# Ten extra products on squared tokens, a higher recording rate for attention pieces, and the second pair's row factors computed apart

## The chip, the cores and the metric

The kernel runs on one core of a Trainium2 chip. Its time is the device time of one execution in microseconds (us); the figure used is the median of several executions. The engines are PE (matmul), DVE (vector), ACT (activation), POOL (GpSimd) and SP, which here only issues DMAs.

## The reference

Attention with normed q and k, then two expert layers, all in fp32:

```
q_n = q / sqrt(mean(q*q) + 1e-6) * g_q          # 4 batches, 12 heads, 448 tokens, 64 wide
k_n = k / sqrt(mean(k*k) + 1e-6) * g_k
a   = softmax(q_n @ k_n.T / 8) @ v              # heads joined: x is 1792 x 768
h   = x @ w_in;  x2 = where(h > 0, h, exp(min(h, 0)) - 1) @ w_out            # 768 -> 2048 -> 768
xn  = x2 / sqrt(mean(x2*x2) + 1e-6) * rms_g
out = (silu(xn @ w_gate) * (xn @ w_val)) @ w_out2                            # 768 -> 1536 -> 768
```

## The kernel before

**Tiles.** Heads are taken two at a time: a pair i (0 to 23) belongs to batch i // 6. A weight or an activation is held as a rounded high part and a low remainder, and a product of two such values is three matmuls of 448 columns (`mm3`). Weights come packed in 8 bytes a value and are unpacked by ACT or POOL and DVE (`w_convert`), kept in DRAM, and split by ACT or POOL and POOL or DVE (`w_split`).

**Stages.** First the lead-in: attention of pairs 0 to 5 alone. Then five stages of expert work: stage 0 is the first experts of batch 0, stage 1 the first experts of batch 1, stage 2 the second experts of both, stages 3 and 4 the same for batches 2 and 3. Attention of later pairs is recorded between the expert units, in pieces. A pair has 15 pieces: four score groups (`s_group`, 0 to 3), eight transposes (`t_bank`) and three parts of the product with v (`pv`). `GOALS` says how many pairs' pieces have been recorded at the end of each stage, and a stage's rate is the pieces still wanted divided by its units (40 in stages 0 and 1). With 12 the rate of stage 0 is (180 - 90) / 40 = 2.25 pieces a unit, and batch 1's last pair, pair 11, is recorded with stage 0's last unit. Stage 1 needs the result of pairs 6 to 11 (`split_x` makes the tiles `xs` from it).

**What a pair does.** `load_tk` brings its q and k rows (`tk`, 480 KB), ACT squares them (`squares`), DVE sums them into `ss`, and `factors` turns sums into the row factors `rr` by some twelve small DVE instructions. `load_rw` brings q and k transposed (`rw`); `prep_q` and `prep_k` split them into high and low parts, after k has been multiplied by its factors spread over the partitions (`rb`). `spread` makes `rb`: for pairs below `FIRST` by eight small matmuls into a PSUM bank, for the others by a DMA to DRAM (`scr`) and two back. Then come scores into a bank, a row maximum on DVE (`nm`), an exponential on ACT with its row sum, transposes through PE, copies, products with v, and a last multiplication by the reciprocal sums, which also travel through DRAM (`rsum`, `rsb`). In the lead-in pairs 1, 3 and 5 put their tiles into storage that is idle then, so the same thing is called `wr` or `gbig` (raw q, k and their parts), `tbig` (p), `ybig` (transposed p, and the tokens of pairs 2 and 3). The tokens of pair 1 and 5 lie in `wr`; those of pairs 0, 4, 6 and all later ones share one tile `tk`, so a load waits until the pair before has been read.

**What sets the order.** Every operation is recorded in a list (`Plan.add`) with a price and the engines that may do it. `Plan.schedule` then plays the list through with these prices, ready operations that were recorded first going first, and gives each engine a fixed order. On the chip each engine works through its own order, and the DMA queue of SP through its own.

**PSUM.** In the lead-in banks 0 to 3 take scores (`r_s`), 4 to 6 transposes (`r_t`), and bank 7 alone takes the spread factors and the output of `pv`. In the order below bank_129 is bank 0 and bank_136 is bank 7.

Of the kernel before, what the change touches and what calls it, by code (L numbers as in the profile page):

```python
# [20 lines left out]
CW = 6  # L21
NF1 = 4
NF2 = 4
FIRST = 1

# [193 lines left out]
def kernel(ctx: ExitStack, tc: tile.TileContext, dims, tok, qk, vr, gq, gk, wst, rmsg, ident_in, out):  # L221
    nc = tc.nc
    B, H, S, D, CF1, CF2 = dims
    NPB = H // 2
# [40 lines left out]
    def size(ap):  # L265
        n = 1
        for s in ap.shape[1:]:
            n *= s
        return n
# [4 lines left out]
    def c_v1(n):  # L274
        return 0.15 + 0.00104 * n
# [7 lines left out]
    def mm(o, l, r, start, stop, price=None):  # L283
        n = size(r)
        plan.add(
            {"pe": (price or max(0.108, n / 2400.0 + 0.017), lambda: T.matmul(o, l, r, start=start, stop=stop))},
            [o], [l, r] + ([] if start else [o]), lag=0.17,
        )
# [70 lines left out]
    def act(dst, src, func, extra=0.0, accum=None, after=None, **kw):  # L359
        if accum is not None:  # L360
            kw["accum_out"] = accum
        plan.add(
            {"a": (c_a(size(src)) + extra, lambda: A.activation(out=dst, in_=src, func=func, **kw))},  # L363
            [dst, accum], [src] + [x for x in kw.values() if hasattr(x, "tensor") and x is not accum], after=after,
        )

    def vop(price, fn, outs, ins, after=None):
        plan.add({"v": (price, fn)}, outs, ins, after=after)
# [4 lines left out]
    def dma(dst, src, nbytes, after=None, soon=False, by="sp"):  # L373
        q, cost = (SP, 0.4) if by == "sp" else (A, 0.2)
        plan.add(
            {by: (cost, lambda: q.dma_start(out=dst, in_=src))},  # L376
            [dst] if dst.name != out.name else [], [src], lag=nbytes / Plan.DMA_RATE, after=after, soon=soon, dma=True,
        )


    ident = sb.tile([P, P], F32, name="ident")
# [52 lines left out]
    r_s, r_t, r_o, r_m = Ring(), Ring(), Ring(), Ring()  # L434
# [93 lines left out]
    def rsqrt(y, x, t, scale, eps):  # L528

        ts(x, x, scale, eps, ALU.mult, ALU.add)  # L530
        yi = y.bitcast(I32)
        ts(yi, x.bitcast(I32), 1, None, ALU.logical_shift_right)
        ts(yi, yi, -1.0, float(0x5F3759DF), ALU.mult, ALU.add)
        ts(x, x, -0.5, None, ALU.mult)
        for _ in range(3):
            tt(t, y, y, ALU.mult, "v")
            tt(t, t, x, ALU.mult, "v")
            stt(y, t, 1.5, y, ALU.add, ALU.mult)

    def tk_of(i):  # L540
        return tks[i % 4 if i < NPB else 0]

    def load_tk(i):
        b, k = divmod(i, NPB)
        if k == 0:
            norms[b] = (r_ss.next(), r_rr.next())
        dma(tk_of(i), tok[i], P * 15 * D * 4)

    def squares(i):

        b, k = divmod(i, NPB)
        tk, ss = tk_of(i), norms[b][0][:, 15 * k:15 * k + 15]
        act(tk, tk, AF.Square)
        tk3 = tk.rearrange("p (t d) -> p t d", d=D)
        vop(c_v1(15 * D), lambda: V.reduce_sum(out=ss, in_=tk3, axis=AX.X), [ss], [tk])

    def factors(b, k0, k1):

        c = slice(15 * k0, 15 * k1)
        ss, rr = norms[b]  # L560
        rsqrt(rr[:, c], ss[:, c], r_sn.next()[:, c], 1.0 / D, 1e-6)

    def spread(i):
# [3 lines left out]
        rr = d["rr"] = norms[b][1][:, 15 * k:15 * k + 15]  # L567
        if i < FIRST:
            rb = d["rb"] = r_o.next()
# [15 lines left out]
    def load_rw(i):  # L585
        dma(l_rw.of(i), qk[i], P * 1024 * 4)

    def load_v(i):
        d = AT.setdefault(i, {})
        t = r_rv.t[i % 2]  # L590
        dma(t, vr[i], P * 512 * 4)
        d["v"] = t.rearrange("p (t d) -> p t d", d=D)

    def prep_q(i):
        d = AT.setdefault(i, {})
        rw, qh, ql = (l.of(i)[:, 0:512] for l in (l_rw, l_qh, l_ql))
        copy(qh, rw)
        tt(ql, rw, qh, ALU.subtract)
        d["q"] = (qh, ql)

    def prep_k(i):
        d = AT[i]
        rw, kh, kl = (l.of(i)[:, 512:1024] for l in (l_rw, l_qh, l_ql))
        stt(rw, rw, gsc[:, 0:1], d["rb"], ALU.mult, ALU.mult)
        copy(kh, rw)
        tt(kl, rw, kh, ALU.subtract)
        d["k"] = (kh, kl)
# [125 lines left out]
    PIECES = 15  # L733

    def tail(i, u):
        t_bank(i, u)
        yield
        if u in (3, 5, 7):
            pv(i, (2, 3) if u == 7 else ((u - 3) // 2,))
            yield  # L740

    def attention():
        load_tk(0)
        load_rw(0)
        load_consts()
        for i in range(1, 4):
            load_tk(i)
        squares(0)
        factors(0, 0, 1)
        spread(0)  # L750
        load_rw(1)
        prep_q(0)
        prep_k(0)
        for i in range(1, NPB):
            squares(i)
            if i + 3 < NPB:
                load_tk(i + 3)
        factors(0, 1, NPB)
        spread(1)
        load_v(0)  # L760
        load_rw(2)
        dma(rg, rmsg, 4096)
        ts(ones, ident, 0.0, 1.0, ALU.mult, ALU.add)
        prep_q(1)
        prep_k(1)
        load_v(1)
        spread(2)
        for i in range(NPB + 1):
            for u in range(8):
                if i < NPB and u % 2 == 0:  # L770
                    s_group(i, u // 2)
                    yield
                if u == 0 and i + 3 < NPB:
                    load_rw(i + 3)
                    spread(i + 3)
                if u == 7 and i + 2 < NPB:
                    prep_q(i + 2)
                    prep_k(i + 2)
                if i > 0:
                    yield from tail(i - 1, u)  # L780
            if 0 < i and i + 1 < NPB:
                load_v(i + 1)

        for i in range(NPB, 2 * NPB):
            load_tk(i)
            squares(i)
        factors(1, 0, NPB)
        load_rw(NPB)
        spread(NPB)
        load_v(NPB)  # L790
        prep_q(NPB)
        prep_k(NPB)
        for i in range(NPB, NPAIR):
            j, n = i + 1, i + NPB
            if n < NPAIR:
                load_tk(n)
            for g in range(4):
                s_group(i, g)
                yield
            if n < NPAIR:  # L800
                squares(n)
                if n % NPB == NPB - 1:
                    factors(n // NPB, 0, NPB)
            if j < NPAIR:
                load_rw(j)
                spread(j)
                load_v(j)
                prep_q(j)
                prep_k(j)
            for u in range(8):  # L810
                yield from tail(i, u)
# [170 lines left out]
            att_step()  # L982

    UNITS = {1: CF1 + (CF1 // NF1) * CD, 2: 2 * CF2 + (CF2 // NF2) * CD}
    GOALS = [12, 19, 24, 24, 24]
    phase(0)
    until(PIECES * NPB)
    phase(1)
    w_ahead()
    for s, (kind, bs) in enumerate(STAGES):  # L990
        goal = PIECES * GOALS[s]
        ahead = STAGES[s + 1] if s + 1 < len(STAGES) else None
        spilled = ahead is not None and ahead[0] == 1 and ahead[1][0] >= 2
        count = UNITS[kind] - (CD if spilled else 0)
        rate = max(goal - pieces["n"], 0) / count
        credit = 0.0
        if s and GOALS[s - 1] >= NPAIR:
            until(NPAIR * PIECES + 1)
            phase(2)
        if kind == 2:  # L1000
            for b in bs:
                if b not in rt:
                    norm(b)
        for step in first_experts(bs) if kind == 1 else second_experts(bs):
            if step == "next":
                if spilled:
                    until(NPAIR * PIECES + 1)
                    for b in ahead[1]:
                        for i in range(b * NPB, b * NPB + NPB):
                            xf = r_tp.next()  # L1010
                            dma(xf, xT[i], P * S * 4)
                            split_x(i, xf)
                continue
            credit += rate
            while credit >= 1.0 and pieces["n"] < goal:
                credit -= 1.0
                att_step()
        until(goal)
        if kind == 1 and s + 1 < len(STAGES) and STAGES[s + 1][0] == 1:
            norm(bs[0])  # L1020
# [6 lines left out]
def layout(inputs):  # L1027
# [19 lines left out]
    for b in range(B):  # L1047
        for hp in range(NPB):
# [11 lines left out]
            for h in range(2):  # L1060
                kk = k[b, 2 * hp + h]
                vv = v[b, 2 * hp + h]
                kx = np.concatenate([kk[384:448], kk], 0)
                if i < FIRST:
                    tok[i, :, 7 + h::2] = kx.reshape(4, P, D).transpose(1, 0, 2)
# [41 lines left out]
```

## Time and profile before

| | us |
|---|---|
| median of 3 executions | 1361.91 (1359.98 to 1365.45) |
| profiled execution | 1362.41 |
| its span | 1360.6 |
| PE busy | 1295.2 (95%) |
| POOL busy | 748.2 (55%) |
| DVE busy | 683.4 (50%) |
| ACT busy | 642.0 (47%) |

PE is busy for nearly the whole span, but not in every part of it: nearly all its gaps lie in the first quarter. A busy time of PE counts matmuls at whatever clock they ran at, so a stretch can be full and slow. In a window's row the numbers are the busy time of each engine and the clock that PE was granted, as a share of the full one.

### The profile page before, as it was taken

What the parts mean: (1) busy time and instruction counts of PE and PEld (TensorE: products, weight loads), DVE (VectorE), ACT (ScalarE), POOL (GpSimd) and SP (SyncE); (2) the same over time, 40 slices, a digit from 0 to 9 for tenths busy, and PEclk for the clock granted to TensorE, in tenths of its full rate; (3) what the DMA queues carried; (4) which work ended last, traced back from release to release, by engine and by line L of the source; (5) the groups of instructions that cost most, each with busy time, mean ns of one, the idle gap of its engine ahead of it and who ended that gap; (6) DMA issues with size and microseconds to landing.
All of it is one profiled execution on the core that took longest, in us unless ns stands there. A gap on an engine that the chain in (4) does not pass through costs nothing.

```text
span 1360.6 us, 17489 instructions
## 1 busy us (share of the span) xinstructions
PE 1295.2 (95%) x6438; PEld 1058.2 (78%) x6438; DVE 683.4 (50%) x997; ACT 642.0 (47%) x1251; POOL 748.2 (55%) x571
## 2 busy tenths in 40 slices
PE   4788989988899999999999999999999999999998
PEld 2345766666577777788888788999999989999998
DVE  5686899886444559953656553102221552132332
ACT  5674767576655666655553452433223532221220
POOL 1354976684564668644564466536345664354450
PEclk9798999989999999999999999999999999999999
DMA  5466777782343445654453425221111211111112
GB/s 182 154 207 216 257 242 237 244 276 82 103 124 109 135 136 167 234 168 145 154 162 121 151 98 175 79 59 47 58 59 47 59 47 58 55 51 59 47 35 81
DMA packets 63142, 174.15 MB, mean 128 GB/s; under 512 B 11200, under 2 KB 20688, under 8 KB 63056
## 3 DMA queue, kind: packets, MB, share of 16 engines
q1 hardware_dynamic: 54064, 163.58, 37.0%
q10 hardware_dynamic: 8992, 9.46, 2.4%
q8 instruction: 50, 0.82, 0.2%
q14 instruction: 36, 0.29, 0.1%
HBM read 137.83 MB, written 35.18 MB: 127 GB/s over the span
## 4 chain that ended last, share of the span: by engine, by line
PE 75%; DVE 9%; DMA 6%; issue 3%; POOL 3%; ACT 2%; SPq 1%; ACTq 0%; DVEq 0%; POOLq 0%
PE bank L295 72%; PE bank L308 3%; DMA wr<-wst 2%; DMA tk<-tok 1%; DVE wt L506 1%; DVE nm L636 1%; DVE xs L355 1%; DMA rb<-scr 1%; DVE nm L638 1%; POOL w L340 1%; DVE wc L355 1%; SPq L376 1%; DVE w L338 1%; POOL gbig L340 1%; POOL ql L340 1%
## 5 line engine op out<-in xcount | busy, mean ns | idle before, releaser
L295 PE MATMUL bank<-xs,w 128*128 128x448 f32 x2880 | 617.9, 370 | 5.7 <-DVE tbig L355 2.8
L295 PEld LDWEIGHTS bank<-xs,w 128*128 128x128 f32 x2880 | 534.3, 188 | 63.4 <-issue 8.9
L295 PE MATMUL bank<-gbig,w 128*128 128x448 f32 x2016 | 437.4, 371 | 8.6 <-POOL gbig L340 4.4
L295 PEld LDWEIGHTS bank<-gbig,w 128*128 128x128 f32 x2016 | 374.4, 189 | 51.5 <-issue 6.8
L340 POOL TENSOR_TENSOR w<-wc,w 128x768 fp32r<-128x768 f32 x156 | 297.0, 1904 | 193.7 <-ACT w L320 187.0
L320 ACT ACTIVATE w<-wc 128x768 fp32r<-128x768 f32 x95 | 80.2, 845 | 191.7 <-PE bank L295 175.1
L340 POOL TENSOR_TENSOR gbig<-tbig,gbig 128x448 fp32r<-128x448 f32 x104 | 126.6, 1218 | 60.1 <-ACT gbig L320 59.0
L636 DVE TENSOR_REDUCE nm<-bank 128x1 f32<-128x448 f32 x168 | 98.1, 616 | 60.8 <-PE bank L295 59.8
L340 POOL TENSOR_TENSOR tbig<-tbig 128x448 f32<-128x448 f32 x67 | 83.7, 1249 | 74.0 <-DVE tbig L355 65.2
L355 DVE SCALAR_TENSOR_TENSOR tbig<-tbig,bank 128x448 f32<-128x448 f32 x64 | 39.3, 616 | 148.1 <-ACT tbig L363 147.9
L324 POOL TENSOR_SCALAR w<-wc 128x768 fp32r<-128x768 f32 x73 | 63.3, 867 | 91.2 <-PE bank L295 73.1
L363 ACT ACTIVATE p<-bank,nm,rr 128x448 f32<-128x448 f32 x126 | 90.1, 720 | 41.5 <-DVE nm L638 35.9
L320 ACT ACTIVATE pt<-bank 128x384 f32<-128x384 f32 (+1 forms) x161 | 69.1, 445 | 51.3 <-PE bank L308 44.1
L308 PEld LDWEIGHTS bank<-ident,p 128*128 128x128 f32 x441 | 54.1, 145 | 48.9 <-issue 26.2
L355 DVE SCALAR_TENSOR_TENSOR wc<-wc,wt 128x768 int32<-128x768 int32 x68 | 78.4, 1152 | 26.3 <-ACT wc L488 18.4
L320 ACT ACTIVATE gbig<-tbig 128x448 fp32r<-128x448 f32 x93 | 53.7, 577 | 71.5 <-DVE tbig L338 46.0
L308 PE MATMUL bank<-ident,p 128*128 128x128 f32 x441 | 76.3, 288 | 11.6 <-ACT p L363 5.6
L363 ACT ACTIVATE tbig<-tbig 128x448 f32<-128x448 f32 x112 | 64.2, 577 | 46.9 <-DVE tbig L338 43.9
L338 DVE TENSOR_TENSOR tbig<-bank,tbig 128x448 f32<-128x448 f32 x48 | 29.7, 621 | 102.9 <-PE bank L295 102.9
L338 DVE TENSOR_TENSOR ybig<-bank,ybig 128x448 f32<-128x448 f32 x72 | 44.5, 620 | 59.0 <-PE bank L295 59.0
L295 PE MATMUL bank<-pt,rv 128*64 128x448 f32 x252 | 70.1, 589 | 3.4 <-ACT pt L320 3.4
L506 DVE TENSOR_SCALAR wt<-wr 128x768 uint16<-128x768 uint16 x68 | 66.7, 980 | 0.4
(96 smaller groups left out, 1195.5 us busy)
## 6 DMA issues: line engine op xcount, KB each, us to landing
wr<-wst SPq DMA_DIRECT2D x68, 768.0 KB
wc<-kept SPq DMA_DIRECT2D x100, 384.0 KB
kept<-wc SPq DMA_DIRECT2D x68, 384.0 KB
rw<-qk SPq DMA_DIRECT2D x21, 512.0 KB
tk<-tok SPq DMA_DIRECT2D x20, 480.0 KB
rv<-vr SPq DMA_DIRECT2D x24, 256.0 KB
out_t<-ybig SPq DMA_DIRECT2D x24, 224.0 KB
rb<-scr ACTq DMA_DIRECT2D x36, 128.0 KB
```

The source lines that it names most:

```text
L295: T.matmul(o, l, r, start=start, stop=stop)
L308: T.transpose(o, i, ident)
L320: alts["a"] = (c_a(n), lambda: A.activation(out=dst, in_=src, func=AF.Copy))
L324: lambda: G.tensor_scalar(out=dst, in0=src, scalar1=1.0, scalar2=0.0, op0=ALU.mult, op1=ALU.add),
L338: alts["v"] = (c_tt(a, b, n), lambda: V.tensor_tensor(out=dst, in0=a, in1=b, op=op))
L340: alts["g"] = (0.25 + 0.0022 * n, lambda: G.tensor_tensor(out=dst, in0=a, in1=b, op=op))
L355: {"v": (c_tt(a, b, size(dst)), lambda: V.scalar_tensor_tensor(out=dst, in0=a, scalar=s, in1=b, op0=op0, op1=op1))},
L363: {"a": (c_a(size(src)) + extra, lambda: A.activation(out=dst, in_=src, func=func, **kw))},
L376: {by: (cost, lambda: q.dma_start(out=dst, in_=src))},
L506: vop(0.15 + 0.00104 * WN, lambda: V.tensor_scalar(out=th, in0=h16, scalar1=0x8000, scalar2=None, op0=ALU.bitwise_and), [th], [h16])
L636: vop(c_v1(S), lambda nm=nm, ot=o[t]: V.tensor_reduce(out=nm, in_=ot, axis=AX.X, op=ALU.max, negate=True), [nm], [o[t]])
L638: vop(0.4, lambda: V.tensor_tensor(out=nm, in0=nm, in1=d["rr"][:, both], op=ALU.mult), [nm], [nm, d["rr"][:, both]])
```

## The change

Three things. The squares of pairs 1 to 5 are each followed by two fp32 products of the identity with the squared tokens (128 x 128 by 128 x 448) into a bank of the transposes' ring; nothing reads them and the next user of the bank writes over them. `FIRST` becomes 2, so pair 1 has its factors spread by PE, and the lead-in is recorded in another order: row factors are computed for pair 1 alone, then for pairs 2 and 3, then for 4 and 5, where they were computed for pairs 1 to 5 together. And `GOALS` of the first two stages go from 12 and 19 pairs to 13.25 and 19.75.

```diff
-FIRST = 1
+FIRST = 2
...
         vop(c_v1(15 * D), lambda: V.reduce_sum(out=ss, in_=tk3, axis=AX.X), [ss], [tk])
 
+        if 0 < i < NPB:
+            o = r_t.next()[:, 0:S]
+            for _ in range(2):
+                mm(o, ident, tk[:, 0:S], True, True, 0.86)
+
...
-        for i in range(1, 4):
-            load_tk(i)
+        load_tk(1)
+        load_rw(1)
+        load_tk(2)
+        load_tk(3)
         squares(0)
         factors(0, 0, 1)
         spread(0)
-        load_rw(1)
         prep_q(0)
         prep_k(0)
-        for i in range(1, NPB):
-            squares(i)
-            if i + 3 < NPB:
-                load_tk(i + 3)
-        factors(0, 1, NPB)
+        squares(1)
+        load_tk(4)
+        factors(0, 1, 2)
         spread(1)
         load_v(0)
+        prep_q(1)
+        prep_k(1)
+        squares(2)
+        squares(3)
+        load_tk(5)
+        factors(0, 2, 4)
         load_rw(2)
+        squares(4)
+        squares(5)
+        factors(0, 4, 6)
         dma(rg, rmsg, 4096)
         ts(ones, ident, 0.0, 1.0, ALU.mult, ALU.add)
-        prep_q(1)
-        prep_k(1)
...
-    GOALS = [12, 19, 24, 24, 24]
+    GOALS = [13.25, 19.75, 24, 24, 24]
...
-        goal = PIECES * GOALS[s]
+        goal = int(PIECES * GOALS[s])
```

The instructions that each engine gets move with it. PE's first instructions of before, after the three of the warm-up: the eight that spread pair 0's factors, then the scores of pair 0 (group 0 into bank_129, group 1 into bank_130 and bank_131).

```order
L295 MATMUL bank_136<-ident,rr_116 64x128 x8
L295 MATMUL bank_129<-qh 128x448
L295 MATMUL bank_129<-qh,ql 128x448
L295 MATMUL bank_129<-ql,qh 128x448
L295 MATMUL bank_130<-qh 128x448
L295 MATMUL bank_131<-qh 128x448
```

And of the changed kernel, where `wr,ident` is the product on pair 1's squares (later pair 5's), `ybig,ident` those on pairs 2 and 3, `tk,ident` that on pair 4.

```order
L286 MATMUL bank_133<-wr,ident 128x448 x2
L295 MATMUL bank_136<-ident,rr_116 64x128 x8
L286 MATMUL bank_134<-ybig,ident 128x448 x2
L286 MATMUL bank_135<-ybig,ident 128x448 x2
L295 MATMUL bank_129<-qh 128x448
L295 MATMUL bank_129<-qh,ql 128x448
L295 MATMUL bank_129<-ql,qh 128x448
L286 MATMUL bank_133<-tk,ident 128x448
L295 MATMUL bank_136<-ident,rr_116 64x128 x8
L286 MATMUL bank_133<-tk,ident 128x448
L286 MATMUL bank_134<-wr,ident 128x448 x2
L295 MATMUL bank_130<-qh 128x448
```

Six products now stand before pair 0's first scores, and the other four, with pair 1's spread, before its second group (bank_130).

ACT's order of before, from the squares of pair 2 and 3 (`ybig`) on: `pj` and `p` are the exponentials of pair 0, `tk<-tk` the squares of pair 4 and then of pair 6.

```order
L363 ACTIVATE ybig<-ybig 128x960 x2
L320 ACTIVATE gbig<-wr 128x512
L320 ACTIVATE qh<-rw 128x512
L363 ACTIVATE tk<-tk 128x960
L363 ACTIVATE wr<-wr 128x960
L363 ACTIVATE pj,sm_119<-bank_129,nm_121,rr_116 128x448
L363 ACTIVATE tk<-tk 128x960
L363 ACTIVATE p,sm_119<-bank_130,nm_121,rr_116 128x448
```

The same place now.

```order
L363 ACTIVATE ybig<-ybig 128x960 x2
L320 ACTIVATE qh<-rw 128x512
L363 ACTIVATE tk<-tk 128x960
L363 ACTIVATE wr<-wr 128x960
L320 ACTIVATE gbig<-wr 128x512
L363 ACTIVATE tk<-tk 128x960
L363 ACTIVATE pj,sm_119<-bank_129,nm_121,rr_116 128x448
L363 ACTIVATE p,sm_119<-bank_130,nm_121,rr_116 128x448
```

The second half of pair 1's preparation (`gbig<-wr`) and the squares of pair 6 have come in front of pair 0's first exponential.

At the end of stage 0, PE of before: the last products of the first three units of stage 1 that can be done without pair 11 (`xs_88`), then pair 11's transposes (`p`), scores of pair 12 (`qh`) and pair 11's first product with v (`pt,rv`).

```order
L295 MATMUL bank_135<-xs_88,w_102 128x448
L308 MATMUL bank_131<-ident,p 128x128 x3
L295 MATMUL bank_129<-qh 128x448
L295 MATMUL bank_129<-qh,ql 128x448
L295 MATMUL bank_129<-ql,qh 128x448
L308 MATMUL bank_131<-ident,p 128x128 x3
L308 MATMUL bank_132<-ident,rs_124 7x128
L308 MATMUL bank_131<-ident,p 128x128 x3
```

The same tail of pair 11 now, from its first transposes on.

```order
L308 MATMUL bank_132<-ident,p 128x128 x3
L295 MATMUL bank_129<-qh 128x448
L295 MATMUL bank_129<-qh,ql 128x448
L295 MATMUL bank_129<-ql,qh 128x448
L295 MATMUL bank_134<-xs_82,w_101 128x448
L295 MATMUL bank_134<-xs_83,w_101 128x448
L295 MATMUL bank_134<-xs_82,w_101 128x448
L308 MATMUL bank_131<-ident,rs_124 7x128
L295 MATMUL bank_134<-xs_84,w_101 128x448
L295 MATMUL bank_134<-xs_85,w_101 128x448
L295 MATMUL bank_134<-xs_84,w_101 128x448
L308 MATMUL bank_132<-ident,p 128x128 x3
```

The tail of pair 11 still comes after stage 1 has begun, but 24 expert matmuls, which all stood ahead of it before, now stand between its steps.

## Rows read from the trace of the kernel before

**Rows 1.** Windows: length, busy us of PE PEld DVE ACT POOL, PEclk, DMA, GB/s.
```profile
13.00:42.00 29.00, 21.34 (x88) 11.41 (x88) 17.90 (x40) 16.66 (x36) 7.25 (x6) 1.00 0.45 148
42.00:52.00 10.00, 4.67 (x16) 2.60 (x15) 6.02 (x11) 4.75 (x11) 4.68 (x6) 0.66 0.67 219
52.00:114.00 62.00, 53.21 (x275) 27.46 (x275) 48.68 (x90) 46.76 (x118) 32.76 (x31) 0.89 0.54 175
...
200.00:326.00 126.00, 117.14 (x583) 84.97 (x581) 106.33 (x143) 85.47 (x173) 91.61 (x67) 0.96 0.71 229
326.00:358.00 32.00, 23.79 (x101) 13.56 (x101) 15.48 (x32) 17.23 (x41) 9.84 (x9) 0.84 0.14 43
358.00:550.00 192.00, 190.06 (x1012) 144.28 (x1010) 114.43 (x170) 117.17 (x261) 124.94 (x96) 1.00 0.44 143
550.00:1360.00 810.00, 805.12 (x3992) 713.02 (x3990) 300.97 (x408) 293.85 (x503) 413.93 (x308) 1.00 0.29 92
```
**Rows 2.** Timeline of PE: start, us, operation, [idle before and its releaser].
```profile
6.00 1.65 PE L286 MATMUL bank<-ident 128*128 128x128 f32 x6 [6.00 <-DMA ident<-ident_in]
13.13 1.97 PE L295 MATMUL bank<-ident,rr 128*64 128x128 f32 x16 [5.48 <-DVE rr L355]
16.61 0.74 PE L295 MATMUL bank<-qh 128*128 128x448 f32 x1 [1.51 <-ACT qh L320]
...
19.19 0.57 PE L295 MATMUL bank<-qh,ql 64*128 64x448 f32 x2
...
38.89 1.66 PE L295 MATMUL bank<-gbig 128*128 128x448 f32 x9
...
47.15 2.19 PE L295 MATMUL bank<-gbig 64*128 64x448 f32 x6 [3.35 <-ACT tbig L363]
...
76.99 0.36 PE L295 MATMUL bank<-qh,ql 64*128 64x448 f32 x2
```
**Rows 3.** Timeline of ACT in the lead-in.
```profile
20.54 0.72 ACT L363 ACTIVATE pj<-bank,nm,rr 128x448 f32<-128x448 f32 x1 [2.19 <-DVE nm L638]
...
21.16 0.19 ACT L363 ACTIVATION_READ_ACCUMULATOR pj<-bank,nm,rr 128x1 f32 x1
...
42.06 0.72 ACT L363 ACTIVATE tbig<-bank,nm,rr 128x448 f32<-128x448 f32 x1 [1.98 <-DVE nm L638]
...
49.38 1.00 ACT L363 ACTIVATE tk<-tk 128x960 f32<-128x960 f32 x1 [1.57 <-DMA tk<-tok]
...
54.81 0.72 ACT L363 ACTIVATE pj<-bank,nm,rr 128x448 f32<-128x448 f32 x1
...
61.46 0.48 ACT L320 ACTIVATE ybig<-bank 128x384 f32<-128x384 f32 x1
```
**Rows 4.** Chain that ended last: start, us, what; of the first 60 us.
```profile
18.67 4.56 DMA tk<-tok
...
33.30 2.56 DMA rb<-scr
```
**Rows 5.** Timeline of DVE in the lead-in.
```profile
11.35 0.17 DVE L355 SCALAR_TENSOR_TENSOR rr<-sn,rr 128x15 f32<-128x15 f32 x1
...
20.35 0.15 DVE L638 TENSOR_TENSOR nm<-nm,rr 128x1 f32<-128x1 f32 x1
...
35.84 0.75 DVE L355 SCALAR_TENSOR_TENSOR wr<-wr,gsc 128x512 f32<-128x512 f32 x1 [2.71 <-DMA rb<-scr]
```
**Rows 6.** Timeline of PE at the end of stage 0.
```profile
335.13 0.28 PE L308 MATMUL bank<-ident,rs 128*7 128x128 f32 x1 [1.66 <-DVE rs L371]
...
344.62 1.79 PE L295 MATMUL bank<-pt,rv 128*64 128x448 f32 x4
...
348.36 0.97 PE L295 MATMUL bank<-pe,rv 64*64 64x448 f32 x4
...
357.25 3.11 PE L295 MATMUL bank<-xs,w 128*128 128x448 f32 x14 [2.69 <-DVE tbig L355]
```
**Rows 7.** Groups of DVE instructions, 114 to 326 us: xcount, busy, mean ns, idle before.
```profile
L638 DVE TENSOR_TENSOR nm<-nm,rr 128x2 f32<-128x2 f32 x17 | 16.6, 976 | 0.0
```

## The prediction

> **What bounds the kernel now.** I read the windows first [rows 1]. From 550 us to the end PE is busy 805.12 of 810 us at full clock, and from 358 to 550 us 190.06 of 192: nothing but PE's work sets the end there, and what PE has behind it by 358 us shifts the end one for one. So the change is worth what it takes from PE's losses before, idle time and time at a lower clock. It touches three places. From 13 to 114 us, the lead-in, PE is busy 21.34 + 4.67 + 53.21 = 79.2 of 101 us, and partly slow. From 200 to 326 us, in stage 0, it is busy 117.14 of 126 at 0.96: 8.9 us idle and some 5 us slow, spread thin. From 326 to 358 us, the turn to stage 1, it is busy 23.79 of 32 at 0.84: 8.2 us idle and 0.16 x 23.8 = 3.8 us slow, 12 us in one place.
>
> The clock column has to be read against durations. It gives 1.00 up to 42 us, but the same score matmul takes 0.57 us at 19 us and 0.36 us at 77 us [rows 2], so the early ones ran at the lower level (1.2 GHz) although the column says full. Around the idle 3.35 us before 47.15 us the column itself falls, to a mean of 0.66 [rows 1, 2].
>
> Why is the lead-in slow? In ACT's timeline [rows 3] pair 0's first exponential is at 20.54 us, pair 1's at 42.06, pair 2's at 54.81. Pair 1 waits for its spread factors: those of pairs 1 to 5 are computed together and go through DRAM, and DVE sits 2.71 us for the last transfer of 2.56 us before it multiplies k at 35.84 us [rows 4, 5]; pair 1's scores start at 38.89 us [rows 2]. Later ACT waits 1.57 us for tokens, until 49.38 us, with exponentials queued behind [rows 3].
>
> **The products.** The trace shows no fp32 product of 128 columns of weights by 448. The warm-up's three by 128 took 1.65 us [rows 2], 0.55 each with the tail; 448 are at most 3.5 x 0.55 = 1.9 us, slow. Two products of half that width by 448, the output with v, take 0.97 us fast and 1.79 slow [rows 6]: a full-width one takes as much if the halves run side by side, half as much if one after the other. So a product lies between 0.49 (fast) and 1.9 us (slow). I take 1.6 slow and 0.85 fast, nearest to the warm-up, which is the same instruction. All ten are 8.5 to 16 us, in a stretch where PE idles more than that, so what counts is whom they delay.
>
> Follow PE's new order. Pair 1's squares end at about 10.3 us as before; its two products run to 13.5, the spread of pair 0 to 15.5 (1.97 us [rows 2]), the four products of pairs 2 and 3 to about 19.5 if the clock rises on the way, to 22 if not. Pair 0's first scores come then, instead of at 16.61 [rows 2]. Three matmuls of scores, one product, pair 1's spread at about 1.0 fast and three more products put the second group near 25 us, some 6 us late. Worse is what ACT now has in front of pair 0's first exponential: the squares of pair 6, whose load into the shared tile must wait until the products have read pair 4's tokens, at about 23.2 us, and takes 4.56 us as it did at 18.67 [rows 4]. With 1.00 us of squares [rows 3] that exponential starts at 28.8 us, 8.3 us late.
>
> Now the return. Pair 1's factors need pair 1's squares alone; DVE does its small instructions at about 0.2 us each [rows 5], between pair 0's. They are ready near 19.3 us, PE has spread them at 22, k is split by 25. So pair 1 waits for no DRAM and takes the next free score banks. Pair 0's last exponentials come, after one more wait for tokens (pair 7's, loaded behind the factors of pairs 2 and 3 on SP), at 36.2 to 38; pair 1's begin at 38.0 instead of 42.06. An exponential with its read-out is 0.72 + 0.19 = 0.9 us, a copy 0.48 [rows 3]: seven of each, 6.3 + 3.2 us with ACT full, put pair 2's first at 47.4 instead of 54.81, 7.4 us early. Two squares and a copy that were done by then before are still to come, 2 x 1.00 + 0.48 = 2.5. That leaves 5 us, which I carry through pairs 2 to 5, where the queue of work is the same. The 24 more small DVE instructions (two more sets of factors), 24 x 0.2 = 4.8 us, are in this trace, beside DVE's waits; without them it would have to wait anyway. SP loses one round trip through DRAM. Lead-in: **-5**, between +8 (nothing given back) and -9 (tokens arrive in time).
>
> **The rate.** Stage 0 records 108 pieces rather than 90, 2.7 a unit; stage 1 then 2.45 instead of 2.63, where PE is full either way. But recorded is not run: in PE's new order 252 score matmuls are past at the first expert matmul of stage 1 instead of 240, of 21 a pair: half a pair more, and pair 11 is still unfinished. Before, its tail stood alone in the window from 326 to 358 us, waiting 1.66 us for DVE in one step [rows 6] and elsewhere for ACT, at a clock that made one group of products with v 1.79 us instead of 0.97 [rows 6]. Now 24 expert matmuls stand between its steps. At 0.2 us each (805.12 us for 3992 [rows 1]) they fill 4.9 us, and with shorter gaps I expect over half of the 3.8 us of slow clock to go. The 2.69 us before 357.25 [rows 6] come after the tail and I leave them. Turn: **-7**, between 0 (the steps wait as long) and -12 (all of it).
>
> Into stage 0 moves half a pair of attention. To PE it is the same work earlier. To DVE it is at most 6 us (72.6 us for six pairs from 13 to 114 us), in a stretch where DVE is busy 106.33 of 126 us [rows 1]; hidden as long as PE is the limit there. **+1**, from 0 to +10.
>
> Here a rule of the Trainium skill speaks against the change. The small product of row maxima and factors takes 0.15 us in the lead-in [rows 5] and 0.976 us on the mean in stage 0 [rows 7]; two groups that move there cost DVE 1.6 us more, for which the +1 has room. The skill's page "SBUF — State Buffer", section "Who interferes with whom", has it that a DVE instruction with two SBUF inputs contends with a GpSimd instruction that reads SBUF, and the loser is blocked for the whole instruction. By that rule the multiplication of k and two or three others would pay 0.8 us too, some 3 us in all, and the sum would be 1354; the first row agrees, the rest no run here shows.
>
> **Sum.** 1362.41 - 5 - 7 + 1 = 1351.4 for the profiled execution, which lies 0.5 above the median: 1351.
>
> **Rivals.**
> 1. *Products not repaid.* The first exponential is 8 us late, PE idles about 4 us before the third score group, and as around 47.15 us [rows 2] the clock falls again, so the products have bought nothing, and the later pairs meet the same waits for tokens. For it: six of ten products stand before any score. Against: pair 1's wait for DRAM is gone. 1362 + 8 - 7 + 1 = 1364.
> 2. *The turn stays.* The 24 matmuls slip in, but the tail waits as long, since it is a chain through DVE, ACT and DRAM; the wait at 335.13 [rows 6] does not depend on PE. Against: PE was slow in it. 1362 - 5 + 1 = 1358.
> 3. *Stage 0 goes with its pieces*, the other side. If DVE and the queues behind it set the pace of stage 0 and not PE, its 212 us (114 to 326) for 90 pieces are 2.36 us a piece, and 18 more cost 42. Later stages give back PE's share alone: at most 79.2 / 90 = 0.88 us a piece, partly slow; I take 0.7, 13 us. 1362 - 5 - 7 + 42 - 13 = 1379. It decides if PE's share of stage 0 falls under some 85%, from 93% [rows 1]. Against: DVE is not full there, and the order moves only half a pair.
> 4. *More everywhere.* The lead-in gains 9, the turn 12, and the thin losses from 200 to 326 us (14 us) shrink by 4: 1337.
>
> **Chances.** Forecast 0.56 (1342 to 1358), rival 1 0.11, rival 2 0.13, rival 3 0.06, rival 4 0.14. What a measurement can tell from no change is 0.5%, 6.8 us, so faster is below 1355: 0.46 of the forecast, 0.14 of rival 4, 0.02 of rival 2, together 0.62. Slower is above 1369: rival 3 and the edges of rival 1 and of the forecast, 0.10. Same: 0.28. A range of 1336 to 1366 leaves out rival 3, some of rival 4 and some of rival 1.
>
> **What would show it.** Pair 0's first exponential near 29 us, pair 2's before 50, and a score matmul of 0.36 us already near 25 us show the lead-in right. Less than 6 us of idle and slow time from pair 11's first transposes after stage 1's first matmul to the end of its last product with v shows the turn. A PE share of stage 0 at or above 92% shows rival 3 wrong. I am wrong if pair 2's first exponential comes after 55 us, or if PE's losses between the lead-in and the turn grow by more than the lead-in gives.

## The result and the profile after

| us | before | changed |
|---|---|---|
| median | 1360.95 (1357.18 to 1365.45, 4 runs) | 1346.86 (1343.64 to 1348.08, 4 runs) |
| profiled execution | 1362.41 | 1348.08 |
| its span | 1360.6 | 1346.3 |
| PE busy | 1295.2 | 1290.9 |
| DVE busy | 683.4 | 693.8 |
| POOL busy | 748.2 | 767.3 |

The ratio is 0.9892, with a 95% interval of 0.9855 to 0.9928: faster by 1.1%. 1351 was forecast, and the measured time lies inside the likeliest case (1342 to 1358). The reasons given for it fared less well.

Windows of the changed kernel, in the columns of [rows 1] (length, busy us of PE PEld DVE ACT POOL, PEclk, DMA, GB/s). The turn has moved 15 us forward, so its 32 us are now those from 311 to 343.

```profile
13.00:42.00 29.00, 22.04 (x101) 12.62 (x100) 24.06 (x73) 15.45 (x34) 5.69 (x5) 0.76 0.58 178
42.00:52.00 10.00, 9.70 (x57) 4.70 (x56) 7.98 (x18) 9.10 (x23) 3.68 (x4) 1.00 0.31 103
52.00:114.00 62.00, 49.75 (x274) 26.50 (x274) 53.18 (x90) 43.07 (x115) 42.42 (x38) 0.91 0.68 220
200.00:326.00 126.00, 121.14 (x632) 89.06 (x629) 104.20 (x142) 85.81 (x178) 97.54 (x71) 1.00 0.64 209
311.00:343.00 32.00, 28.29 (x138) 20.39 (x137) 22.59 (x42) 22.59 (x50) 17.04 (x15) 0.95 0.38 114
343.00:535.00 192.00, 188.09 (x1004) 139.21 (x1002) 107.83 (x162) 118.25 (x270) 127.20 (x97) 1.00 0.44 140
535.00:1346.30 811.30, 805.21 (x3985) 715.58 (x3984) 306.67 (x407) 295.65 (x494) 406.22 (x300) 1.00 0.29 91
```

The turn: 3.7 us idle and 0.05 x 28.3 = 1.4 slow, 5.1 us, where [rows 1] had 12.0. From 200 to 326 us PE is busier than before and at full clock. After the turn it is idle 3.9 of 192 us, where it was 1.9: something is given back there.

PE's timeline in the changed kernel's lead-in, to set beside [rows 2].

```profile
10.79 3.35 PE L286 MATMUL bank<-wr,ident 128*128 128x448 f32 x4 [2.72 <-ACT wr L363]
14.07 1.36 PE L295 MATMUL bank<-ident,rr 128*64 128x128 f32 x16
15.36 3.27 PE L286 MATMUL bank<-ybig,ident 128*128 128x448 f32 x8
18.13 0.71 PE L295 MATMUL bank<-qh 128*128 128x448 f32 x1
18.68 0.36 PE L295 MATMUL bank<-qh,ql 128*128 128x448 f32 x1
...
23.41 0.47 PE L295 MATMUL bank<-qh 64*128 64x448 f32 x2
...
27.27 0.47 PE L295 MATMUL bank<-qh 64*128 64x448 f32 x1 [2.79 <-ACT pj L363]
...
29.46 0.57 PE L295 MATMUL bank<-qh,ql 64*128 64x448 f32 x2
...
31.91 2.16 PE L295 MATMUL bank<-gbig 128*128 128x448 f32 x4 [1.51 <-ACT p L363]
```

A product appears as two records: the first two products take 3.35 us (1.67 each), the next four 3.27 (0.82 each), so the clock rises to its upper level (2.4 GHz) near 15 us, and a score matmul takes 0.36 us at 18.68. Pair 1's scores start at 31.91 us instead of 38.89. But PE waits 2.79 us for ACT, and from 28.9 us the matmuls take 0.57 us again, at the lower level (1.2 GHz), until about 41 us.

ACT's timeline there, beside [rows 3]: the squares of pair 6 (`tk<-tk`), then the first exponentials of pairs 0, 1 and 2.

```profile
25.51 1.00 ACT L363 ACTIVATE tk<-tk 128x960 f32<-128x960 f32 x1 [3.02 <-DMA tk<-tok]
26.42 0.71 ACT L363 ACTIVATE pj<-bank,nm,rr 128x448 f32<-128x448 f32 x1
...
37.28 0.72 ACT L363 ACTIVATE tbig<-bank,nm,rr 128x448 f32<-128x448 f32 x1
...
47.92 0.72 ACT L363 ACTIVATE pj<-bank,nm,rr 128x448 f32<-128x448 f32 x1 [0.56 <-DVE rs L349]
```

Pair 0 is 5.9 us later than before, pair 1 4.8 us earlier, pair 2 6.9 us earlier.

PE at the end of stage 0, where [rows 6] had pair 11's tail alone.

```profile
321.68 0.97 PE L295 MATMUL bank<-pt,rv 128*64 128x448 f32 x4
...
323.20 1.49 PE L295 MATMUL bank<-xs,w 128*128 128x448 f32 x6
324.62 0.97 PE L295 MATMUL bank<-pt,rv 128*64 128x448 f32 x4
...
325.83 1.48 PE L295 MATMUL bank<-xs,w 128*128 128x448 f32 x6
327.23 1.05 PE L295 MATMUL bank<-pt,rv 128*64 128x448 f32 x4
328.21 0.97 PE L295 MATMUL bank<-pe,rv 64*64 64x448 f32 x4
...
338.24 3.17 PE L295 MATMUL bank<-xs,w 128*128 128x448 f32 x9 [3.54 <-DVE tbig L355]
```

Expert matmuls (`xs,w`) stand between pair 11's products with v, these take 0.97 to 1.05 us where [rows 6] had 1.79, and no wait shows until the last product. What is left is one wait of 3.54 us, the successor of the 2.69 in [rows 6].

### The profile page after: what moved, and what is told of

Read it like the earlier page. It is cut to its first block, busy times and chain, and to the rows that moved or that the text cites. A ratio compares the mean times of both kernels' runs of the same rounds, so it can differ in the third digit from the quotient of the medians.

```text
span 1346.3 us, 17602 instructions
## 1 busy us (share of the span) xinstructions
PE 1290.9 (96%) x6474; PEld 1057.8 (79%) x6474; DVE 693.8 (52%) x1010; ACT 641.0 (48%) x1253; POOL 767.3 (57%) x582
## 4 chain that ended last, share of the span: by engine, by line
PE 76%; DVE 8%; POOL 5%; issue 2%; DMA 2%; ACT 1%; ACTq 0%; POOLq 0%; DVEq 0%; SPq 0%
PE bank L295 73%; PE bank L308 4%; DVE wc L355 2%; DVE nm L641 1%; POOL w L340 1%; DMA wr<-wst 1%; POOL w L324 1%; DVE wt L506 1%; POOL wt L501 1%; DVE nm L643 1%; DVE gbig L338 1%; POOL gbig L340 1%; POOL ql L340 0%; DVE tbig L355 0%; POOL tbig L340 0%
## 5 line engine op out<-in xcount | busy, mean ns | idle before, releaser
L340 POOL TENSOR_TENSOR w<-wc,w 128x768 fp32r<-128x768 f32 x163 | 308.0, 1890 | 196.0 <-ACT w L320 188.7
L320 ACT ACTIVATE w<-wc 128x768 fp32r<-128x768 f32 x86 | 72.6, 845 | 175.1 <-PE bank L295 173.4
L340 POOL TENSOR_TENSOR tbig<-tbig 128x448 f32<-128x448 f32 x68 | 87.0, 1279 | 69.5 <-DVE tbig L355 65.0
L324 POOL TENSOR_SCALAR w<-wc 128x768 fp32r<-128x768 f32 x82 | 74.1, 904 | 91.2 <-PE bank L295 82.7
L641 DVE TENSOR_REDUCE nm<-bank 128x1 f32<-128x448 f32 x168 | 97.9, 616 | 47.4 <-PE bank L295 47.0
L355 DVE SCALAR_TENSOR_TENSOR tbig<-tbig,bank 128x448 f32<-128x448 f32 x64 | 39.4, 616 | 159.0 <-ACT tbig L363 158.9
L355 DVE SCALAR_TENSOR_TENSOR wc<-wc,wt 128x768 int32<-128x768 int32 x68 | 81.8, 1203 | 28.0 <-ACT wc L488 22.8
L355 DVE SCALAR_TENSOR_TENSOR ybig<-bank,ybig 128x448 f32<-128x448 f32 x48 | 29.9, 623 | 77.7 <-PE bank L295 77.7
L355 DVE SCALAR_TENSOR_TENSOR tbig<-tbig 128x448 f32<-128x448 f32 x48 | 55.5, 1157 | 25.7 <-ACT tbig L363 25.4
```

The lines of the kernel that those rows point to most:

```text
L320: alts["a"] = (c_a(n), lambda: A.activation(out=dst, in_=src, func=AF.Copy))
L324: lambda: G.tensor_scalar(out=dst, in0=src, scalar1=1.0, scalar2=0.0, op0=ALU.mult, op1=ALU.add),
L340: alts["g"] = (0.25 + 0.0022 * n, lambda: G.tensor_tensor(out=dst, in0=a, in1=b, op=op))
L355: {"v": (c_tt(a, b, size(dst)), lambda: V.scalar_tensor_tensor(out=dst, in0=a, scalar=s, in1=b, op0=op0, op1=op1))},
L641: vop(c_v1(S), lambda nm=nm, ot=o[t]: V.tensor_reduce(out=nm, in_=ot, axis=AX.X, op=ALU.max, negate=True), [nm], [o[t]])
```

## The experiments

All were timed in five rounds beside the kernel before. They are read against one table. Its losses are worked out from each run's PE timeline: the time passed, minus the work PE has done by then at full-clock prices read from it (0.2045 us for a matmul of 448 columns with 128 rows of weights, 0.103 with 64, 0.225 for a product with v, 0.12 for a transpose, nothing for the products, the spread and the warm-up). "Ahead" is the number of score matmuls that PE's fixed order has in front of stage 1's first expert matmul. Losses are of one execution, and the times of a kernel's executions, where it had six or more, lie 6 to 16 us apart: that of e7 was its slowest of twelve, that of e9 its fastest.

| run | ahead | loss to 60 | to 125 | to 300 | to 375 | to 550 | profiled | ratio, 95% |
|---|---|---|---|---|---|---|---|---|
| before | 240 | 44.5 | 64.4 | 95.3 | 115.2 | 124.6 | 1362.41 | 1 |
| changed | 252 | 39.2 | 61.0 | 88.8 | 98.7 | 111.5 | 1348.08 | 0.9892 (0.9855 to 0.9928) |
| e1 changed again | 252 | 38.1 | 58.4 | 86.5 | 97.1 | 109.2 | 1341.90 | 0.9891 (0.9864 to 0.9918) |
| e2 thin products | 252 | 38.4 | 60.1 | 89.1 | 99.0 | 111.1 | 1343.60 | 0.9886 (0.9859 to 0.9913) |
| e3 no products | 252 | 39.7 | 62.6 | 88.7 | 98.7 | 110.8 | 1347.71 | 0.9897 (0.9873 to 0.992) |
| e4 none on pair 4 | 252 | 38.6 | 59.7 | 86.5 | 96.3 | 108.4 | 1340.68 | 0.9888 (0.9861 to 0.9915) |
| e5 old goals | 246 | 38.8 | 60.5 | 89.2 | 104.4 | 113.5 | 1347.98 | 0.9921 (0.9888 to 0.9955) |
| e6 goals alone | 246 | 45.7 | 65.2 | 97.0 | 115.3 | 126.3 | 1365.73 | 1.0032 (1.0008 to 1.0056) |
| e7 order alone | 246 | 39.3 | 65.0 | 92.3 | 110.2 | 119.6 | 1359.00 | 0.9943 (0.992 to 0.9965) |
| e8 products alone | 252 | 44.3 | 61.3 | 96.7 | 109.9 | 119.3 | 1351.79 | 0.9957 (0.9934 to 0.998) |
| e9 thin products alone | 252 | 43.5 | 61.3 | 93.3 | 105.0 | 114.1 | 1346.60 | 0.9959 (0.9934 to 0.9984) |
| e10 factors alone | 240 | 35.2 | 53.9 | 93.0 | 113.6 | 123.0 | 1355.58 | 0.9986 (0.9962 to 1.0009) |
| e11 factors through DRAM | 240 | 40.6 | 58.8 | 89.7 | 119.2 | 129.5 | 1369.62 | 1.0035 (1.0011 to 1.006) |
| e12 higher rate | 252 | 39.4 | 60.8 | 87.5 | 102.1 | 117.2 | 1351.79 | 0.9957 (0.9935 to 0.9979) |

After 550 us PE is nearly full in every run, and yet the same working gives a loss there of 7 to 15 us, which does not go with the kernel: 11.4 us in the changed kernel, 7.6 in e1, which is the same kernel. Most of the difference is PE's pace. Windows of the changed kernel, then of e1:

```profile
850.00:950.00 100.00, 100.00 (x486) 90.83 (x485) 13.21 (x22) 34.35 (x59) 49.15 (x38) 1.00 0.19 56
```
```profile
850.00:950.00 100.00, 100.00 (x495) 92.67 (x494) 14.33 (x23) 34.18 (x59) 47.28 (x36) 1.00 0.18 55
```

Busy throughout and with the clock column at 1.00, PE does 486 matmuls in one execution and 495 in the other. Why is not known. So a single profiled time says less than the losses up to 550 us and the ratios.

**The products.** e1 is the changed kernel again, for the same chip. e2 gives the products 8 columns at the old price, so that every engine's order is the same and PE has next to no work from them:

```diff
-                mm(o, ident, tk[:, 0:S], True, True, 0.86)
+                mm(o[:, 0:8], ident, tk[:, 0:8], True, True, 0.86)
```

e3 takes the products out, and the plan is made anew; e4 takes out the two on pair 4:

```diff
-        if 0 < i < NPB:
+        if 0 < i < NPB and i != 4:
```

> The changed kernel itself, as an anchor for the runs beside it. Theory A (lead-in 5 us from pair 1's early start, turn to stage 1 worth 7 us) and every rival: 1347 us, ratio to before 0.989, with a narrower interval.

> Same order on every engine, but each of the ten products has 8 columns instead of 448, so PE spends almost nothing on them. Theory A (the products only delay pair 0's first scores): scores of pair 0 near 16 us instead of 18.1, first exponential 1 to 2 us earlier, time 1344 to 1346. Rival B (the products pay by the clock): score matmuls before 30 us take 0.57 us instead of 0.36, PE is slow until about 45 us, time 1349 to 1352. Rival C (nothing of it reaches the end, because tokens are waited for in any case): 1347, within 1.

> The changed kernel with its products taken out, so the order is planned anew; by the order the turn is as in the changed kernel. Theory A: 1344 to 1346. Rival B (clock): 1349 to 1352. Rival C: 1347.

> Eight products, none on pair 4, whose tokens lie in the tile that pair 6's tokens are loaded into. Theory A (that load stands ahead of pair 0's first exponential on ACT): load issued some 1 us earlier (after DVE's sum of pair 4), first exponential at 25.4 instead of 26.4, time 1346. Rival C (DVE's sum holds the load as long): 1347, no difference that can be told.

Medians: e1 1346.38, e2 1346.99, e3 1347.36, e4 1343.93 us, before 1361.50. Rival C came out for e2 and e3; e4's median lies below both of its forecasts, but its ratio is no other than that of e1. Neither the products' time nor their place costs or pays anything that can be told. Without them PE waits for pair 0's factors in their place. PE and ACT of e3:

```profile
13.23 1.98 PE L295 MATMUL bank<-ident,rr 128*64 128x128 f32 x16 [5.38 <-DVE rr L355]
16.72 0.74 PE L295 MATMUL bank<-qh 128*128 128x448 f32 x1 [1.51 <-ACT qh L320]
...
26.97 0.74 PE L295 MATMUL bank<-qh 64*128 64x448 f32 x1 [4.16 <-ACT pj L363]
```
```profile
23.51 0.99 ACT L363 ACTIVATE tk<-tk 128x960 f32<-128x960 f32 x1
...
26.10 0.72 ACT L363 ACTIVATE pj<-bank,nm,rr 128x448 f32<-128x448 f32 x1 [1.60 <-DVE nm L638]
```

The scores start 1.4 us earlier than in the changed kernel, but pair 0's first exponential only 0.3 us, less than two executions of one kernel differ (26.42 us in the changed kernel, 25.18 in e1): without the products it waits for DVE, whose order has pair 1's multiplication of k and the factors of two later pairs in front of the last step of the row maximum.

**The rate and the order, each alone.** e5 is the changed kernel with the old goals, e6 the kernel before with the new ones, e7 the new order of the lead-in with neither products nor goals, e8 the products alone. e5's edit, e7's further one, and e6's and e8's in the kernel before:

```diff
-    GOALS = [13.25, 19.75, 24, 24, 24]
+    GOALS = [12, 19, 24, 24, 24]
...
-        if 0 < i < NPB:
-            o = r_t.next()[:, 0:S]
-            for _ in range(2):
-                mm(o, ident, tk[:, 0:S], True, True, 0.86)
```
```diff
-    GOALS = [12, 19, 24, 24, 24]
+    GOALS = [13.25, 19.75, 24, 24, 24]
```
```diff
+        if 0 < i < NPB:
+            o = r_t.next()[:, 0:S]
+            for _ in range(2):
+                mm(o, ident, tk[:, 0:S], True, True, 0.86)
```

> The changed kernel with GOALS 12 and 19 as before. In its order 15 expert matmuls stand between the steps of pair 11's tail (24 in the changed kernel, 0 before). Theory A (what counts is what stands between the steps): the turn keeps more than half of its gain, time 1349 to 1351. Rival D (the recording rate gives the turn): it is as before, 12 us of loss there, time 1354.

> The kernel before with only the new GOALS. Its order puts 21 expert matmuls between the steps of pair 11's tail; the lead-in is as before. Theory A: turn gains 6, time 1354 to 1356. Rival D: the rate gives all, 1348 to 1350. Rival E (the gain of the change is that of another order by chance, spread over stage 0): anything from 1350 to 1365, with the turn's loss not below 10 us.

> The new lead-in (pair 1's factors by PE and alone), without the products and with the old GOALS. Theory A: lead-in 5 us, turn 4 us by 15 matmuls between the steps: 1349 to 1353. Rival B (products needed for the clock): lead-in gains nothing, 1356.

> The kernel before with the products alone. 15 expert matmuls stand between the steps of pair 11's tail. Theory A: the products delay pair 0 by 2 to 3 us, which stays, the turn gains 4: 1359 to 1361. Rival B (clock): lead-in 4 us shorter, 1353 to 1355.

Medians: e5 1348.37, e6 1363.10, e7 1351.61, e8 1354.06 us, before 1360.14. The rate alone gains nothing (ratio 1.0032); on top of the order it gains 4 to 6 us (e7 to e3, by the medians and by the ratios; the two ran on different chips), and on top of order and products 2 to 4 us that are not clear of noise (e5 to e1). The order alone gives 8, over half of the whole. And the products, worth nothing in e2 and e3, gain 6 us by themselves.

Against what was expected: e5 is just faster than theory A had it, and its turn (300 to 375 us) keeps about half of the gain (15.2 us, with 19.9 before and 9.9 in the changed kernel). e7's time is that of A, with less from the turn than A had (17.9 us). e6 missed A and D; its time and its turn of 18.3 us are what rival E, another order by chance, allowed. e8 missed A, which had the turn's gain at 4 us (it is 7) and a delay of 2 to 3 us that stays; B's time came out but not its reason, as the lead-in is not shorter (44.3 us at 60 us, 44.5 before).

The turn of e6, in PE's timeline, shows why more recorded pieces did not help.

```profile
332.85 1.48 PE L295 MATMUL bank<-xs,w 128*128 128x448 f32 x6 [1.61 <-ACT tbig L363]
...
345.81 1.92 PE L295 MATMUL bank<-xs,w 128*128 128x448 f32 x8 [0.75 <-POOL xs L340]
...
354.54 1.49 PE L295 MATMUL bank<-xs,w 128*128 128x448 f32 x3 [6.01 <-DVE tbig L355]
```

The wait after the tail, 2.69 us in [rows 6], is 6.01 us here: a good part of what the tail gained went into it.

**Four that tell why.** e9 is e8 with products of 8 columns. e10 has pair 1's factors computed alone and spread by PE, in the kernel before:

```diff
-FIRST = 1
+FIRST = 2
...
         for i in range(1, NPB):
             squares(i)
             if i + 3 < NPB:
                 load_tk(i + 3)
-        factors(0, 1, NPB)
+            if i == 1:
+                factors(0, 1, 2)
+        factors(0, 2, NPB)
```

e11 is the changed kernel with `FIRST = 1`, e12 with `GOALS = [14.5, 21, 24, 24, 24]`.

> The kernel before with the ten products, but of 8 columns at the old price, so the fixed order of every engine is that of the run with products alone (1354.06 us, ratio 0.9957), and PE has next to no work from them. Theory A: the products act only through their price in the plan, which puts half a pair of attention ahead at the turn: 1354, from 1351 to 1357, ratio 0.994 to 0.997, and the turn (325 to 375 us) loses 10 to 11 us as with full products. Theory B: their time on PE, or the clock that they keep up, is what helps: 1360 to 1363, ratio 0.999 to 1.001.

> The kernel before with one step: pair 1's row factors are computed alone and spread by PE; no products, old goals, all else recorded where it was. At the turn as much attention is ahead as before (240 score matmuls). Theory A: this step is what gives the lead-in's gain, and the turn's gain comes with the order that is not here: PE's loss at 60 us falls from 44 to 38 or 39, the turn's stays at 12 to 16, and the time is 1355 to 1358, ratio 0.995 to 0.998. Theory B: the gain of the lead-in needs the preparation of pair 1 recorded ahead of the later squares and the other factors: loss at 60 us 42 to 44, time 1359 to 1362, ratio 0.999 to 1.001.

> The changed kernel with pair 1's factors computed alone but spread through DRAM as before. By the plan the attention ahead at the turn is that of the kernel before (240 score matmuls instead of 252), though the goals are the new ones. Theory A: what counts at the turn is what the plan puts there, and what counts in the lead-in is that pair 1 waits for its own squares alone, not who spreads: loss at 60 us about 40 and a turn of 12 to 16 us, time 1352 to 1356, ratio 0.993 to 0.996. Theory B: the spread by PE is what the lead-in gains from: loss at 60 us 43 to 45, time 1358 to 1362, ratio 0.997 to 1.001. Theory C: the new rate alone makes the turn short: turn under 9 us, time below 1350.

> The changed kernel with goals of 14.5 and 21 pairs instead of 13.25 and 19.75. Theory A: the rate itself is worth nothing beyond the place of pair 11's tail, which is already ahead: 1345 to 1349, ratio 0.988 to 0.991, the turn 7 to 9 us. Theory B: the rate is worth its pieces, and half as much again gives 2 to 4 us more: 1342 to 1344, ratio below 0.987. Theory C: stage 0 takes longer by its pieces: 1352 or more, the loss between 125 and 325 us 5 us above the changed kernel's 28.

Medians: e9 1354.61, e10 1359.74, e11 1365.14, e12 1354.25 us, before 1360.44.

e9 settles the products: the same gain with hardly any work behind them, so it is their price in the plan. Far from the edit, it puts 252 score matmuls ahead at the turn instead of 240, and the turn (300 to 375 us) loses 11.7 us instead of 19.9.

e10 has the best lead-in of all, 9 us better at 60 us, and gains nothing that can be told. Theory A was right about the lead-in, B's time came out. PE and DVE of e10, and DVE of the kernel before, at the spread factors of pair 6:

```profile
139.31 3.35 PE L295 MATMUL bank<-gbig,w 128*128 128x448 f32 x8 [6.39 <-POOL gbig L340]
```
```profile
135.74 0.75 DVE L355 SCALAR_TENSOR_TENSOR rw<-rw,gsc,rb 128x512 f32<-128x512 f32 x1 [5.27 <-DMA rb<-scr]
```
```profile
131.70 0.75 DVE L355 SCALAR_TENSOR_TENSOR rw<-rw,gsc,rb 128x512 f32<-128x512 f32 x1 [8.02 <-DMA rb<-scr]
```

In both the next round trip through DRAM holds DVE up; before, PE still had expert work of its own, and in e10, ahead by 9 us, it runs dry behind POOL, which waits for DVE. At 300 us e10 is at 93.0 us of loss, before at 95.3. The changed kernel's DVE has no wait for a DMA from 100 to 210 us. Its PE has its long wait earlier, for ACT's copy of a lead-in pair's transposed p; from 60 to 125 us it loses 21.8 us, before 19.9. PE of the changed kernel:

```profile
113.92 3.36 PE L295 MATMUL bank<-ybig,rv 128*64 128x448 f32 x8 [4.44 <-ACT ybig L320]
```

e11 shows the turn from its other side. All that the lead-in gains (4 us at 60 us, 6 at 300) is there, and the kernel is slower than before. Its order has 240 ahead, the tail stands alone, and the wait behind it is the long one. PE of e11:

```profile
314.84 0.97 PE L295 MATMUL bank<-pt,rv 128*64 128x448 f32 x2 [2.48 <-ACT pt L320]
...
333.43 0.38 PE L308 MATMUL bank<-ident,rs 128*7 128x128 f32 x1 [1.69 <-DVE rs L371]
...
358.74 1.49 PE L295 MATMUL bank<-xs,w 128*128 128x448 f32 x3 [6.04 <-DVE tbig L355]
```

I had expected 1352 to 1356 (A) or 1358 to 1362 (B); it missed both, since neither reckoned with the long wait, nor with the one of 2.48 us at 314.84 us.

e12 missed A's 1345 to 1349 and B's 1342 to 1344. C's time came out, but not for C's reason: from 125 to 300 us it loses 26.7 us, no more than the changed kernel. With 252 ahead its tail is covered, but it has the long wait again. PE, then DVE of e12:

```profile
341.67 1.49 PE L295 MATMUL bank<-xs,w 128*128 128x448 f32 x3 [6.04 <-DVE tbig L355]
```
```profile
337.65 1.14 DVE L641 TENSOR_REDUCE nm<-bank 128x1 f32<-128x448 f32 x2
338.72 0.69 DVE L338 TENSOR_TENSOR ql<-rw,qh 128x512 fp32r<-128x512 f32 x1
339.33 1.75 DVE L643 TENSOR_TENSOR nm<-nm,rr 128x2 f32<-128x2 f32 x1
341.01 1.67 DVE L355 SCALAR_TENSOR_TENSOR tbig<-tbig,bank 128x448 f32<-128x448 f32 x3
```

And DVE of the changed kernel:

```profile
334.03 2.57 DVE L338 TENSOR_TENSOR w<-wc,w 128x768 fp32r<-128x768 f32 x1 [1.81 <-POOL w L324]
336.52 1.14 DVE L641 TENSOR_REDUCE nm<-bank 128x1 f32<-128x448 f32 x2
337.58 0.60 DVE L355 SCALAR_TENSOR_TENSOR tbig<-tbig,bank 128x448 f32<-128x448 f32 x1
```

The instruction that PE waits for (`tbig<-tbig,bank`, which frees a bank) comes at once after the row maxima in the changed kernel, and two instructions later, 2.44 us, in e12. So in these two the wait's length follows from what DVE's fixed order has in front of that instruction; no run changes that order alone.

## Why the prediction was right, and where it was not

By the losses in the table, changed against before:

| step | predicted | measured |
|---|---|---|
| lead-in | -5 | -5.3 at 60 us, -3.4 at 125 us |
| stage 0 (125 to 300) | +1 | -3.1 |
| turn (300 to 375) | -7 | -10.0; by windows 12.0 to 5.1, -6.9 |
| from 375 to 550 | 0 | +3.4 |
| sum | -11 | -13.1; profiled executions -14.3 |

That the sum is so near is partly luck: with the lead-in read at 125 us, the rows are off by +2, -4, -3 and +3 us.

**The turn** went as the prediction had it: the expert matmuls stand between the tail's steps, and the tail's products with v take 0.97 to 1.05 us, the time of the full clock. That its cause is how much attention the order has ahead rests on a row of kernels: where 240 score matmuls are ahead, 300 to 375 us lose 19.9, 20.6 and 29.5 us; with 246, 15.2 to 18.3; with 252, 9.8 to 14.6. e9 shows it without any work added, though its order differs elsewhere too. What the prediction mis-sized is who puts it there: it gave the step to the rate. The rate alone (e6) gains nothing. Order, products' price and rate each change the plan, and the plan's outcome at the turn does not follow from the goals: e11 has the new goals and 240.

**The wait behind the tail** was left at 2.69 us. It was 3.54, and in other orders 6.0: a term that I took for fixed differs among the orders by 3.4 us, half of the gain that I gave to the turn.

**The lead-in** gave its 5 us at 60 us, by the steps that were traced: 26.42, 37.28 and 47.92 us for 28.8, 38.0 and 47.4. Pair 6's tokens took 3.5 us to land rather than 4.56, from the load's issue at 22.00 us to 25.51. Two steps in it were wrong. That the products delay pair 0: without them (e3) its first exponential is at 26.10, since ACT's squares and DVE's factors hold it there anyway; rival 1 priced 8 us for what costs nothing. And "what PE has behind it by 358 us shifts the end one for one" holds but for PE's pace after 550 us, and 5 us at 60 us are not yet 5 us at 358: e10 had 9 and kept 2 at 300. Something that comes with the lead-in's new order does last until the turn: the nine kernels that have it have lost 86.5 to 92.3 us by 300 us, the four with the old one (before, e6, e8, e9) 93.3 to 97.0, with about 7 us between the means. How much of that is the lead-in itself, and how much another order in stage 0, is open.

**The clock.** The products raised it by 15 us, and it fell after the 2.79 us wait, as rival 1 said; so they bought nothing, and e2 shows they cost nothing.

**Stage 0** lost less rather than more, and that DVE's work there rose cannot be told: from 125 to 300 us DVE is busy 145.9 us before, 153.1 in the changed kernel and 144.7 in e1. From 114 to 311 us DVE's groups in the changed kernel, beside [rows 7] (xcount, busy, mean ns, idle before):

```profile
L643 DVE TENSOR_TENSOR nm<-nm,rr 128x2 f32<-128x2 f32 x17 | 12.4, 732 | 0.1
L355 DVE SCALAR_TENSOR_TENSOR rw<-rw,gsc,rb 128x512 f32<-128x512 f32 x7 | 9.8, 1395 | 1.3 <-DMA rsum<-rt 1.3
```

The multiplication of k takes 1395 ns on the mean, with 0.75 us where it stands alone ([rows 5], the same form on `wr`). This agrees with the rule that spoke against the change, of the Trainium skill's page "SBUF — State Buffer", section "Who interferes with whom", that a DVE instruction with two SBUF inputs contends with a GpSimd instruction that reads SBUF. But it took 989 ns on the mean before and 1046 ns in e1, and the product of row maxima fell from 976 to 732 ns, so what the change itself added cannot be told. The 1354 worked out by the rule was further off than 1351. Rival 3 is wrong by its own sign: PE's share is 121.14 of 126 us from 200 to 326 us, 96%. Rival 4's thin losses did shrink, by some 3 us of its 4 (125 to 300 us). Why stage 0 lost less no run isolates.

**After the turn** the prediction had nothing, with stage 1 "where PE is full either way". From 375 to 550 us PE loses 12.8 us instead of 9.4, with new, short waits (the longest 1.71 us, for POOL). The table says what brings them: the six kernels with the old goals lose 9.1 to 9.4 us there, the seven with the new ones 10.3 to 12.8, and e12, with higher ones, 15.1; e5 (9.1) differs from the changed kernel in the goals alone. That is a price of the rate which the prediction left out.

**The signs of being wrong** did not come: pair 2's first exponential is at 47.92 us, before 55, and the losses between the lead-in and the turn shrank.

## What to carry to other kernels

Where a planner sets the order, an edit acts through its price as well as through its work: time it once with the price and without the work (e9 against e8, e2 against e1) before giving it a cause. A gain at the start counts only from the last point at which another wait, here a round trip through DRAM and a tail that must be finished, could have absorbed it. And a hand-over between stages is worth checking on the order itself: count what stands ahead of it, and look at what each engine's order has in front of the instruction that is waited for.

## What the runs showed of the hardware

An fp32 product of 128 x 128 by 128 x 448 took 1.67 us at the lower clock and 0.82 at the upper. A product of row maxima and factors for two columns took 1.75 us in the rows of e12 above, beside a POOL subtraction on SBUF, and 0.15 us for one column in [rows 5], while no POOL instruction ran. PEclk read 0.76 from 13 to 42 us in the changed kernel and 1.00 in the kernel before, where a score matmul took 0.57 us at 19 us and 0.36 at 77 us [rows 2]: in the lead-in that column did not tell the clock, and the durations had to be asked. And with PEclk at 1.00 and PE busy throughout, matmuls of the same kernel ran 2% slower in one execution than in another (486 and 495 matmuls in 100 us).
